# GpSimd's port work waits for planned VectorE work, LayerNorm statistics in larger groups, and a new order, in a spectral filter with a product-key expert layer

## The chip, the cores and the metric

One core of a Trainium2 chip runs the kernel. The metric is device microseconds of one execution, the median of several runs. A profiled execution gives the trace; its engines are PE (TensorE, with PEld for its weight loads), DVE (VectorE), ACT (ScalarE), POOL (GpSimd) and SP (SyncE, which issues the DMAs).

## The reference

```python
def _A_ref(x, w_r, w_i):
    X = rfft2(x, axes=(-2, -1))
    X = X * (w_r + 1j * w_i)
    return irfft2(X, s=(S, D), axes=(-2, -1))

def _B_ref(x, w_q, k1, k2, u, v):
    q = einsum("nd,dhc->nhc", x, w_q)
    s1 = einsum("nhd,ed->nhe", q[..., :dk], k1)
    s2 = einsum("nhd,ed->nhe", q[..., dk:], k2)
    # best key of each half for each head, K = 1
    i1, i2 = argmax(s1), argmax(s2)
    e = i1 * E + i2
    g = softmax over the one chosen score
    act = gelu(einsum("nd,nhkd->nhk", x, u[e]))
    return einsum("nhk,nhk,nhkd->nd", g, act, v[e])

xn = layernorm(x, axis=-1)
out = x + _A_ref(xn, w_r, w_i) + _B_ref(xn, w_q, k1, k2, u, v)
```

Here it is shortened. S = 2048 rows of D = 576; 32 heads, dk = 128, E = 8 keys in each half, 64 experts. All is float32.

## The kernel before

The 2048 rows lie in 16 tiles of 128. The kernel has these stages; the names are those that the trace shows, a tile name with several purposes is told.

*Statistics and forward DFT over rows, 16 tiles.* `ln(t, n)` makes the mean and variance of `n` tiles: BN_STATS on two halves of 288 columns (`st`) and an aggregate (`mv`) on VectorE, or, for the five tiles in `SA`, two passes over `XN` on ACT. Then ACT takes the square root for the whole group, VectorE its reciprocal, and one Newton step follows in three instructions, in `rr`: with a group of one or two tiles as three TENSOR_SCALAR for each tile, one column wide; with a group of more than two as three SCALAR_TENSOR_TENSOR for all its columns. Before the change the groups are of one, one and then seven times two tiles. `folds(t)` folds each row onto itself, two sums and differences of 289 columns (`t`) and then folds of 145 and 288 columns (`A`, whose tile is `A2`), on VectorE and GpSimd; ACT makes `Rs`, the row transform scaled by the tile's `rr`, and `yl`, a copy of some columns. `dft128(t)` multiplies `A` and `yl` by `Rs` on TensorE, and ACT copies the result to `AB` and `ABL`; a last difference for `ABL` is VectorE's.

*The folded keys.* `fold_part` reduces w_q with the keys, 32 tiles `w` of 576 KB that stream through five buffers; TensorE multiplies each by `KP`. These matmuls stand between those of the first stage and after them.

*The rest of the spectral branch.* `d_fwd` and `s_fwd` finish the forward transform (`c`, `s`), `s_mul(g)` multiplies by the weights: two products from PSUM on VectorE (`t<-banks,wx,Wt`), sums `y` on GpSimd, the high half `yh` on ACT, the low half `yh<-y,yh` on GpSimd, and `yl` on ACT. `s_inv(g)` is the inverse over rows, in 16 parts, and `d_inv(t)`, `fin(t)` the inverse over columns and the sum of both branches.

*The expert branch.* `x_t(r)` loads and scales `xT`, in two halves, the low one on VectorE or GpSimd; `scores(r)`, `route(r)` and `combine(r)` make the scores of two tiles, find the best key (`mx`, `w`, `MT` on VectorE) and the expert's weight (`MT`, `CZ` on GpSimd). `allmax` makes a scale from all partitions, through TensorE and an `mxr` on VectorE.

*What sets the order.* `body` doesn't issue instructions as it meets them. `_Engine` records each into a `_Plan`; `add` notes its planned cost, what it depends on, and in `op.port` whether it uses the port that VectorE and GpSimd are taken to share: every GpSimd instruction with an input, and a VectorE instruction with two inputs in SBUF or a copy or TENSOR_SCALAR from SBUF to SBUF. `forward` then plans: engine by engine it takes, of the instructions that are ready, the one with the highest priority, and lets only one user of the port run at a time. The priorities are a table, `RANK`, with one number for each recorded piece of work, 1319 before and 1284 after. `issue` calls the recorded functions in the planned order, so every instruction has the trace line of that call, L540 (L542 after). Each engine takes its own instructions in that order; between engines only data holds them. SyncE issues the DMAs, in that order too.

```python
    LOADS = ((0, 2), (2, 2), (4, 4), (8, 4), (12, 4))
```

These are the pieces in which `x` comes in, in tiles: first tile, count. They are the same before and after.

Of the kernel before, what the change touches and what calls it, by code (L numbers as in the profile page):

```python
# [32 lines left out]
def _consts():  # L33
# [102 lines left out]
    859, 1293, 1261, 1295, 1300, 1304, 1298, 1260, 593, 475, 479, 478, 895, 1174, 1177, 1005, 868, 805, 590,  # L136
    1187, 555, 893, 762, 927, 588, 543, 587, 892, 558, 410, 526, 537, 991, 728, 1049, 1022, 781, 857, 236,
    509, 1211, 758, 1168, 419, 658, 982, 981, 488, 1184, 957, 636, 1219, 985, 835, 218, 255, 943, 926, 986,
    679, 561, 722, 620, 611, 628, 862, 300, 709, 1026, 1079, 710, 517, 1042, 594, 1114, 1136, 1208, 856, 631,
    897, 319, 321, 880, 1266, 365, 1274, 723, 1169, 727, 888, 860, 915, 138, 145, 838, 858, 474, 606, 433,  # L140
    1011, 583, 626, 579, 815, 609, 373, 894, 342, 407, 343, 748, 445, 941, 1061, 1217, 655, 798, 973, 90, 189,
    741, 896, 415, 470, 1210, 1170, 356, 1220, 1037, 944, 178, 115, 913, 1013, 402, 673, 1244, 293, 751, 235,
    760, 922, 642, 601, 598, 354, 640, 610, 368, 299, 1178, 674, 1085, 416, 1267, 1252, 157, 314, 1202, 1110,
    1016, 731, 1151, 369, 1289, 494, 1086, 1032, 287, 317, 1138, 242, 198, 1082, 1108, 401, 666, 1247, 1130,
    1120, 816, 495, 597, 392, 1155, 530, 539, 965, 1097, 1087, 831, 869, 1175, 961, 186, 162, 219, 227, 199,
    1109, 1071, 1088, 570, 779, 1183, 1044, 306, 291, 1286, 847, 216, 372, 998, 371, 914, 1100, 1124, 1221,
    1056, 384, 763, 524, 566, 571, 387, 1212, 569, 318, 1215, 607, 480, 596, 463, 267, 483, 501, 667, 689,
    417, 1119, 1222, 386, 843, 575, 284, 175, 1111, 656, 533, 535, 577, 580, 261, 1066, 1053, 1281, 776, 546,
    338, 367, 333, 337, 545, 481, 1095, 1040, 366, 1272, 700, 531, 323, 266, 1041, 527, 891, 484, 840, 619,
    678, 615, 618, 536, 326, 269, 962, 1259, 390, 786, 828, 827, 1190, 809, 1065, 1265, 435, 425, 428, 599,  # L150
    540, 427, 426, 1080, 948, 1029, 547, 632, 1195, 845, 308, 116, 789, 792, 693, 1018, 1076, 604, 613, 396,
    884, 271, 32, 57, 311, 310, 329, 257, 156, 1189, 273, 500, 440, 1280, 756, 106, 1067, 97, 817, 270, 518,
    442, 456, 498, 1307, 1314, 952, 1309, 901, 1291, 1294, 1292, 1305, 767, 614, 247, 721, 379, 1299, 208,
    1303, 1205, 1301, 281, 1296, 521, 1297, 73, 1306, 394, 1229, 160, 1232, 355, 877, 1171, 459, 883, 890,
    1150, 210, 1310, 324, 1149, 209, 1283, 229, 1312, 105, 1248, 91, 1246, 165, 1250, 232, 904, 563, 882, 336,
    560, 265, 237, 1245, 1131, 989, 225, 681, 250, 950, 221, 1161, 58, 796, 233, 1179, 11, 1034, 919, 829,
    974, 477, 441, 214, 516, 204, 514, 278, 176, 378, 854, 173, 1023, 823, 234, 461, 790, 172, 783, 341, 476,
    1126, 289, 1139, 813, 253, 272, 254, 1268, 169, 898, 1256, 1092, 344, 1239, 429, 1009, 334, 292, 777, 161,
    268, 1165, 812, 550, 361, 1207, 1240, 395, 1050, 240, 376, 141, 765, 629, 328, 305, 617, 552, 670, 348,
    573, 239, 1159, 803, 900, 572, 899, 933, 578, 554, 553, 842, 397, 352, 231, 263, 163, 353, 262, 1253, 984,  # L160
    264, 109, 936, 290, 983, 1311, 312, 450, 801, 1308, 1209, 799, 761, 1313, 750, 680, 773, 1302, 844, 1039,
    720, 807, 657, 302, 804, 918, 430, 104, 103, 102, 100, 1288, 13, 154, 1132, 638, 639, 313, 1129, 616, 222,
    230, 970, 223, 806, 309, 205, 260, 1104, 1199, 246, 1135, 301, 244, 248, 834, 1060, 512, 602, 872, 1121,
    468, 431, 403, 486, 454, 833, 1101, 1064, 89, 93, 92, 1255, 203, 940, 277, 1007, 276, 586, 411, 1015, 771,
    811, 1198, 362, 249, 224, 695, 1063, 1269, 754, 283, 256, 393, 770, 715, 707, 641, 711, 1141, 1271, 1, 4,
    1069, 422, 1047, 385, 1096, 841, 1001, 1033, 1006, 1083, 787, 251, 228, 785, 932, 243, 325, 94, 1146, 968,
    226, 887, 213, 279, 280, 1287, 136, 132, 129, 127, 121, 126, 449, 1185, 755, 744, 574, 1193, 954, 589,
    1081, 1273, 643, 1200, 902, 96, 1181, 171, 177, 380, 282, 351, 295, 258, 259, 1073, 1036, 1249, 742, 824,
    5, 0, 938, 886, 1270, 1070, 955, 346, 917, 978, 556, 874, 423, 404, 1012, 977, 170, 168, 375, 340, 349,
    339, 595, 511, 976, 1162, 942, 793, 928, 3, 2, 906, 660, 207, 193, 206, 994, 374, 238, 327, 110, 303, 820,  # L170
    1290, 80, 88, 81, 79, 59, 153, 627, 1218, 649, 582, 653, 464, 544, 1062, 1000, 1238, 1194, 956, 1137, 152,
    775, 381, 167, 496, 331, 1106, 513, 399, 1014, 725, 1031, 1243, 724, 691, 133, 1197, 735, 1204, 1206, 621,
    697, 646, 335, 534, 360, 747, 759, 716, 714, 851, 992, 949, 1254, 245, 1052, 307, 830, 510, 489, 447, 708,
    706, 797, 538, 448, 1241, 174, 1123, 1214, 128, 87, 86, 1264, 1213, 275, 485, 166, 608, 668, 1318, 149,
    130, 124, 1231, 122, 123, 729, 907, 1167, 460, 444, 740, 418, 929, 947, 1285, 1234, 1004, 912, 52, 1057,
    414, 150, 591, 451, 873, 520, 482, 1230, 652, 732, 567, 622, 519, 101, 99, 951, 1019, 347, 939, 802, 692,
    971, 832, 1038, 794, 1107, 1164, 492, 462, 1075, 1228, 412, 83, 712, 452, 644, 696, 528, 525, 737, 694,
    931, 733, 1051, 191, 33, 1003, 357, 77, 82, 146, 1115, 769, 60, 499, 76, 562, 358, 1237, 117, 95, 190,
    202, 201, 197, 988, 1116, 1020, 1098, 585, 1224, 1196, 1142, 1024, 1276, 676, 808, 960, 113, 969, 75, 140,
    766, 389, 654, 388, 457, 434, 635, 634, 746, 1074, 1117, 84, 44, 630, 1226, 1172, 911, 1017, 1058, 662,  # L180
    605, 600, 1021, 1166, 453, 1284, 772, 664, 885, 144, 78, 505, 800, 1227, 879, 446, 432, 734, 1089, 909,
    1133, 503, 85, 413, 1182, 1192, 188, 114, 98, 1203, 866, 184, 532, 187, 1160, 1143, 108, 1242, 134, 151,
    288, 65, 135, 768, 810, 934, 975, 703, 1275, 1277, 865, 875, 1258, 1102, 853, 995, 37, 1030, 1046, 111,
    504, 472, 743, 881, 304, 274, 633, 739, 424, 749, 548, 1282, 139, 753, 1235, 1316, 1103, 1025, 469, 1257,
    522, 1145, 107, 112, 502, 864, 458, 690, 1093, 1223, 945, 684, 730, 719, 780, 69, 1233, 1068, 837, 192,
    147, 119, 814, 612, 64, 467, 120, 663, 542, 62, 55, 61, 54, 53, 143, 63, 867, 788, 958, 471, 846, 523,
    515, 1002, 819, 1154, 1027, 848, 964, 45, 778, 1090, 158, 757, 581, 736, 1216, 1262, 1263, 1043, 980,
    1077, 1099, 861, 1315, 764, 559, 466, 493, 871, 491, 159, 1173, 1191, 487, 1176, 437, 686, 541, 726, 738,
    1122, 717, 704, 155, 164, 74, 72, 46, 71, 70, 997, 1188, 1201, 465, 1225, 568, 473, 1140, 1112, 398, 497,
    1054, 923, 1078, 421, 196, 67, 1158, 252, 822, 391, 1317, 529, 551, 370, 320, 405, 345, 200, 142, 1186,  # L190
    508, 791, 420, 795, 889, 905, 996, 687, 406, 752, 294, 675, 443, 490, 1279, 1278, 35, 36, 818, 1045, 438,
    821, 924, 34, 56, 935, 377, 946, 1094, 937, 38, 15, 436, 1028, 718, 42, 47, 993, 439, 920, 1091, 921, 41,
    40, 637, 972, 1251, 39, 31, 903, 400, 603, 930, 659, 26, 27, 698, 1127, 1113, 43, 25, 1008, 702, 908, 870,
    705, 24, 23, 699, 990, 910, 211, 22, 825, 359, 576, 685, 623, 66, 68, 999, 1156, 1163, 30, 28, 826, 688,
    1153, 925, 564, 10, 148, 322, 1134, 1152, 17, 16, 713, 316, 315, 624, 1128, 7, 6, 1236, 1055, 1147, 8, 9,
    878, 651, 650, 683, 1059, 14, 12, 863, 1144, 1035, 20, 21, 1180, 855, 682, 661, 1118, 181, 179, 876, 1125,
    1148, 19, 180, 625, 565, 701, 1010, 849, 50, 49, 669, 979, 967, 51, 29, 836, 506, 507, 584, 784, 183, 131,
    549, 953, 959, 212, 48, 1157, 1048, 557, 1084, 774, 125, 182, 409, 966, 963, 18, 118, 648, 455, 852, 672,
    592, 1072, 220, 330, 987, 839, 137, 185, 408, 383, 382, 677, 671, 217, 215, 665, 1105, 916, 297, 296, 850,
# [1069 lines left out]
```

## Time and profile before

| | before |
|---|---|
| median of 3 runs | 222.05 us (221.85 to 222.1) |
| the profiled execution | 222.02 us |
| its span, first to last instruction | 220.1 us |
| granted TensorE clock | 0.992 |
| busy: PE, DVE, ACT, POOL | 194.9, 187.4, 130.5, 115.0 us |
| DMA: bytes | 48.12 MB |

A row of the trace names the line, the engine, the operation, what is written from what, and the shape; `x8` counts instructions. A timeline row has the start and the time from the first start to the last end, with the releaser of the idle time before it in brackets. Instructions overlap on an engine, so a group's time can be shorter than the sum of its instructions, and the distance between two starts tells what one more of them takes.

### The profile page before, as it was taken

How to read it: one execution, taken by the hardware profiler on the slowest of the kernel's cores; microseconds unless marked ns; L12 is line 12 of the kernel's file. 1: busy time of each engine (PE TensorE's matmuls, PEld its weight loads, DVE VectorE, ACT ScalarE, POOL GpSimd, SP SyncE). 2: the span in 40 equal slices, each digit the busy share in tenths (PEclk: the TensorE clock that was granted, in tenths of full speed). 3: DMA queues.
4: the chain of work that ended last, by engine and by line, in shares of the span. 5: the costliest groups of instructions: out<-in, count | busy, mean ns of one | idle time of the engine just before them, and what ended most of it. 6: DMA issues, size and time to landing. Idle time of an engine off the chain costs nothing.

```text
span 220.1 us, 6024 instructions
## 1 busy us (share of the span) xinstructions
PE 194.9 (89%) x2324; PEld 131.4 (60%) x2324; DVE 187.4 (85%) x457; ACT 130.5 (59%) x308; POOL 115.0 (52%) x153
## 2 busy tenths in 40 slices
PE   0179978989899999999999999969989999999990
PEld 0168557667656775657467465446555568877860
DVE  1999999971784967874899999999999999999980
ACT  2267989898857895849627934955635532213320
POOL 4644653602509840673416634867737239568760
PEclk9999999999999999999999999999999999999996
DMA  6999999999999999998224260201000000575466
GB/s 206 394 429 416 331 416 348 312 360 362 389 415 344 420 409 418 418 442 311 91 81 123 103 190 0 60 3 42 33 3 1 0 4 0 134 183 121 114 153 165
DMA packets 17020, 48.12 MB, mean 219 GB/s; under 512 B 2144, under 2 KB 8544, under 8 KB 16224
## 3 DMA queue, kind: packets, MB, share of 16 engines
q1 hardware_dynamic: 16992, 47.74, 61.1%
q8 instruction: 18, 0.29, 0.5%
q14 instruction: 10, 0.08, 0.1%
HBM read 43.01 MB, written 4.72 MB: 217 GB/s over the span
## 4 chain that ended last, share of the span: by engine, by line
PE 57%; DVE 29%; ACT 4%; issue 3%; DMA 3%; POOL 0%; ACTq 0%; DVEq 0%
PE banks L540 57%; DVE t L540 6%; DVE w L540 4%; DVE MT L540 4%; DVE A L540 3%; DVE st L540 2%; DVE rr L540 2%; DVE ABL L540 2%; DMA XN<-in_x_dram 2%; DVE AB L540 1%; ACT xT L540 1%; DMA w<-in_wq_dram 1%; DVE mx L540 1%; ACT xf L540 1%; DVE mm__96 L540 1%
## 5 line engine op out<-in xcount | busy, mean ns | idle before, releaser
L540 PE MATMUL banks<-MU,xT 128*128 128x512 f16 x192 | 45.7, 379 | 0.0
L540 PE MATMUL banks<-c,AB 128*128 128x145 f16 (+2 forms) x320 | 37.8, 252 | 0.0
L540 POOL TENSOR_TENSOR A<-t 128x287 f32<-128x287 f32 (+2 forms) x42 | 29.5, 722 | 15.6 <-DVE t L540 10.3
L540 POOL TENSOR_TENSOR y<-t,t 128x289 f32<-128x289 f32 x32 | 23.2, 748 | 22.7 <-DVE t L540 22.1
L540 PEld LDWEIGHTS <-xT 128*128 128x128 f16 x224 | 20.7, 98 | 23.2 <-issue 0.9
L540 DVE SCALAR_TENSOR_TENSOR t<-banks,wx,Wt 128x578 f32<-128x578 f32 x32 | 24.2, 810 | 3.9 <-PE banks L540 3.7
L540 POOL TENSOR_TENSOR yh<-y,yh 128x578 f16<-128x578 f32 x16 | 22.8, 1436 | 8.4 <-ACT yh L540 6.7
L540 PE MATMUL banks<-Rs,yl 128*99 128x128 f32 x64 | 12.0, 321 | 14.3 <-ACT Rs L540 11.8
L540 POOL TENSOR_TENSOR xT<-xf,xT 128x640 f16<-128x640 f32 x10 | 14.0, 1402 | 14.5 <-ACT xf L540 13.5
L540 ACT ACTIVATE AB<-banks 128x512 f32<-128x512 f32 (+1 forms) x32 | 18.8, 591 | 2.1 <-PE banks L540 1.8
L540 PEld LDWEIGHTS banks<-Rs,yl 128*99 128x99 f32 x64 | 8.6, 186 | 19.0 <-ACT Rs L540 14.2
L540 PE MATMUL banks<-w,KP 128*32 128x288 f32 x256 | 19.7, 414 | 0.1
L540 ACT ACTIVATE yh<-banks 128x290 f32<-128x290 f32 (+1 forms) x16 | 7.3, 458 | 20.8 <-PE banks L540 20.7
L540 PE MATMUL banks<-c,ABL 99*128 99x289 f16 (+1 forms) x64 | 18.8, 298 | 0.4 <-DVE ABL L540 0.4
L540 PEld LDWEIGHTS banks<-c,AB 128*128 128x128 f32 x128 | 17.9, 190 | 1.2 <-issue 0.5
L540 PE MATMUL banks<-Rs,A 128*128 128x128 f32 x128 | 18.5, 299 | 0.0
L540 DVE TENSOR_REDUCE MT<-w 128x128 bf16<-128x896 bf16 (+1 forms) x16 | 18.1, 1136 | 0.0
L540 PE MATMUL banks<-A,s 64*64 64x289 f32 x256 | 18.0, 411 | 0.0
L540 PEld LDWEIGHTS banks<-Rs,A 128*128 128x128 f32 x128 | 17.4, 214 | 0.9 <-issue 0.9
L540 PEld LDWEIGHTS <-AB 128*128 128x128 f16 x192 | 17.2, 147 | 0.1
L540 ACT ACTIVATE xT<-xf,bx 128x640 f16<-128x640 f32 x16 | 13.0, 821 | 5.6 <-PE banks L540 5.5
L540 POOL TENSOR_TENSOR t<-XN 128x289 f32<-128x289 f32 x14 | 11.9, 864 | 8.4 <-DVE A L540 4.2
(127 smaller groups left out, 417.8 us busy)
## 6 DMA issues: line engine op xcount, KB each, us to landing
w<-in_wq_dram SPq DMA_DIRECT2D x32, 576.0 KB, 6.8
xf<-in_xT_dram SPq DMA_DIRECT2D x16, 320.0 KB, 5.6
Wt<-in_W_dram SPq DMA_DIRECT2D x8, 578.0 KB, 6.7
out_dram<-XN SPq DMA_DIRECT2D x32, 144.0 KB, 2.5
XN<-in_x_dram SPq DMA_DIRECT2D x3, 1154.0 KB, 10.7
s<-in_s_dram SPq DMA_DIRECT2D x16, 192.0 KB, 5.1
XN<-in_xd_dram SPq DMA_DIRECT2D x2, 1152.0 KB, 9.7
XN<-in_xd_dram SPq DMA_DIRECT2D x1, 2304.0 KB, 12.3
```

The costliest lines, as they stand in the source:

```text
L540: fn(*[x.place() if isinstance(x, _Ps) else x for x in args], **{k: x.place() if isinstance(x, _Ps) else x for k, x in kw.items()})
```

## The change

Three things change.

The groups of `ln` become those of `LOADS`. With them go the instructions that work on a group: the square root, the reciprocal, and, where a group has four tiles, the Newton step.

`issue` keeps, for each VectorE instruction that it has issued, the planned end with some time added. For each GpSimd instruction that uses the port it looks for the last VectorE instruction with such an end no later than its own planned start, and adds a dependency on it. It adds no second dependency on the same instruction.

`RANK` is replaced as a whole, so that the order on each engine is another.

```diff
 RANK = (
-    859, 1293, 1261, 1295, 1300, 1304, 1298, 1260, 593, 475, 479, 478, 895, 1174, 1177, 1005, 868, 805, 590,
...
+    464, 1220, 901, 1223, 1261, 1268, 1219, 1221, 391, 444, 431, 691, 894, 879, 874, 922, 835, 890, 883, 839,
...
 )
-    def issue(self):
+    def issue(self, tc):
...
+        sync = mybir.DependencyInfo(mybir.DependencyClass.Sync, mybir.DependencyReason.DATA)
+        queue, held = [], None
         for i in order:
-            for fn, args, kw in ops[i].calls:
-                fn(*[x.place() if isinstance(x, _Ps) else x for x in args],
-                   **{k: x.place() if isinstance(x, _Ps) else x for k, x in kw.items()})
+            o = ops[i]
+            for fn, args, kw in o.calls:
+                ins = fn(*[x.place() if isinstance(x, _Ps) else x for x in args],
+                         **{k: x.place() if isinstance(x, _Ps) else x for k, x in kw.items()}).ins
+            if o.eng == "vector":
+                queue.append((start[i] + o.cost + 225, ins))
+            elif o.eng == "gpsimd" and o.port:
+                first = [v for t, v in queue if t <= start[i] + 30]
+                if first and first[-1] is not held:
+                    held = first[-1]
+                    tc.add_manual_dep(ins, held.name, sync, reason="port")
...
-        plan.issue()
+        plan.issue(tc)
...
-    for t, n in ((0, 1), (1, 1), (2, 2), (4, 2), (6, 2), (8, 2), (10, 2), (12, 2), (14, 2)):
+    for t, n in ((0, 2), (2, 2), (4, 4), (8, 4), (12, 4)):
         ln(t, n)
         for i in range(t, t + n):
             folds(i)
```

Counted over the program, VectorE has 382 rows of such an order instead of 412, ACT 266 instead of 275, and TensorE and GpSimd the same work.

The first instructions on VectorE, from the first that waits for `x`. The numbers in the names are buffers: `A2_0` and `A2_1` are here tiles 0 and 1.

Before:

```order
L540 TENSOR_TENSOR t1_1_99<-XN_67 128x289
L540 BN_STATS st_0_97<-XN_67 128x6 x2
L540 BN_AGGR mv_87<-st_0_97 128x2
L540 BN_STATS st_0_97<-XN_67 128x6
L540 RECIPROCAL rr_86<-rr_86 128x1
L540 TENSOR_TENSOR A2_1_101<-t1_1_99 128x145
L540 TENSOR_SCALAR rr_86<-rr_86 128x1
L540 TENSOR_TENSOR A2_1_101<-t1_1_99 128x145
L540 TENSOR_SCALAR rr_86<-mv_87,rr_86 128x1
L540 TENSOR_TENSOR t1_0_98<-XN_67 128x289
L540 TENSOR_SCALAR rr_86<-rr_86 128x1
```

After the change, from the same place up to the first pair's `rr`:

```order
L542 TENSOR_TENSOR t_0_98<-XN 128x289
L542 BN_STATS st_97<-XN 128x6 x2
L542 BN_AGGR mv<-st_97 128x2
L542 TENSOR_TENSOR A_1_101<-t_1_99 128x145
L542 BN_AGGR mv<-st_97 128x2
L542 BN_STATS st_97<-XN 128x6
L542 RECIPROCAL rr<-rr 128x2
L542 BN_STATS st_97<-XN 128x6
L542 TENSOR_SCALAR rr<-rr 128x1 x2
L542 TENSOR_TENSOR t_1_99<-XN 128x289
L542 BN_AGGR mv<-st_97 128x2
L542 TENSOR_SCALAR rr<-mv,rr 128x1 x2
```

Ahead of the rows shown stand four BN_STATS, a fold of 145 columns and an aggregate, and after them two more TENSOR_SCALAR on `rr`. The Newton step of the first tile stood after two BN_STATS; it now stands after eight, for two tiles together. The first such step over four tiles, that of tiles 4 to 7, comes some 35 rows later.

The first matmuls on TensorE, from the first on. `Rs_0` and `Rs_1` are two buffers that even and odd tiles take in turn, `A2_0` to `A2_3` four that go round the tiles, and `w_0` is the first tile of the folded keys.

Before:

```order
L540 MATMUL banks_66<-Rs_0_104,yl_0_106 99x2x8x8 x2
L540 MATMUL banks_66<-Rs_0_104,A2_0_100 128x128 x4
L540 MATMUL banks_66<-Rs_1_105,yl_1_107 99x2x8x8 x2
L540 MATMUL banks_66<-Rs_0_104,yl_0_106 99x2x8x8 x2
L540 MATMUL banks_66<-Rs_0_104,A2_2_102 128x128 x4
L540 MATMUL banks_66<-Rs_1_105,A2_1_101 128x128 x4
L540 MATMUL banks_66<-w_0_119,KP_73 32x288 x4
L540 MATMUL banks_66<-Rs_1_105,yl_1_107 99x2x8x8 x2
L540 MATMUL banks_66<-Rs_1_105,A2_3_103 128x128 x4
```

After:

```order
L542 MATMUL banks_66<-Rs_1_105,yl_1_107 99x2x8x8 x2
L542 MATMUL banks_66<-Rs_0_104,yl_0_106 99x2x8x8 x2
L542 MATMUL banks_66<-Rs_1_105,A2_1_101 128x128 x4
L542 MATMUL banks_66<-Rs_0_104,A2_0_100 128x128 x4
L542 MATMUL banks_66<-Rs_1_105,yl_1_107 99x2x8x8 x2
L542 MATMUL banks_66<-w_0_119,KP_73 32x288 x4
L542 MATMUL banks_66<-Rs_1_105,A2_3_103 128x128 x4
L542 MATMUL banks_66<-Rs_0_104,yl_0_106 99x2x8x8 x2
L542 MATMUL banks_66<-Rs_1_105,yl_1_107 99x2x8x8 x2
L542 MATMUL banks_66<-Rs_0_104,A2_2_102 128x128 x4
L542 MATMUL banks_66<-Rs_1_105,A2_1_101 128x128 x4
```

Tiles 0, 1 and 3 come first; the ninth row is the `yl` of tile 5, and stands ahead of the tenth, the four matmuls of tile 2. Before, all of tile 2 stood ahead of tiles 3, 4 and 5.

GpSimd in the middle of the inverse over rows, with the engines whose semaphores each instruction waits for.

Before:

```order
L540 TENSOR_TENSOR y_0_131<-t1_0_98,t2_0_108 128x289 [waits DVE_49,Pool_49]
L540 TENSOR_TENSOR y_0_131<-t2_0_108,t1_0_98 128x289
L540 TENSOR_TENSOR CZ_80<-MT_79,CZ_80 128x2x64 [waits Activation_49]
L540 TENSOR_TENSOR MT_79<-MT_79,mk_70 128x128
L540 TENSOR_TENSOR yh_0_133<-y_0_131,yh_0_133 128x578 [waits PE_49,Activation_49]
L540 TENSOR_TENSOR y_1_132<-t2_1_109,t1_1_99 128x289 [waits DVE_49]
L540 TENSOR_TENSOR y_1_132<-t1_1_99,t2_1_109 128x289
L540 TENSOR_TENSOR yh_1_134<-y_1_132,yh_1_134 128x578 [waits Activation_49]
```

After:

```order
L542 TENSOR_TENSOR y_0_131<-t2_0_108,t1_0_98 128x289 [waits DVE_49,Pool_49]
L542 TENSOR_TENSOR y_0_131<-t1_0_98,t2_0_108 128x289 [waits DVE_49]
L542 TENSOR_TENSOR CZ_80<-MT_79,CZ_80 128x2x64 [waits DVE_49]
L542 TENSOR_TENSOR MT_79<-MT_79,mk_70 128x128 [waits DVE_49]
L542 TENSOR_TENSOR yh_0_133<-y_0_131,yh_0_133 128x578 [waits DVE_49,Activation_49]
L542 TENSOR_TENSOR y_1_132<-t1_1_99,t2_1_109 128x289 [waits DVE_49]
L542 TENSOR_TENSOR y_1_132<-t2_1_109,t1_1_99 128x289 [waits DVE_49]
L542 TENSOR_TENSOR yh_1_134<-y_1_132,yh_1_134 128x578 [waits DVE_49,PE_49,Activation_49]
```

The order here is nearly the same. Each row now names VectorE: of GpSimd's 143 computing instructions 52 waited for VectorE before, and 128 do after.

127 rows, old and new, of the table RANK are left out of this document.

## The prediction

> **What bounds the kernel now.** The sums of the page and its chain of waits come first.
>
> ```profile
> PE 194.9 (89%) x2324; PEld 131.4 (60%) x2324; DVE 187.4 (85%) x457; ACT 130.5 (59%) x308; POOL 115.0 (52%) x153
> PE 57%; DVE 29%; ACT 4%; issue 3%; DMA 3%; POOL 0%; ACTq 0%; DVEq 0%
> ```
>
> TensorE is busy for 194.9 of 220.1 us and VectorE for 187.4; the chain runs over both and never over GpSimd. An average hides the stages, so the busy time by windows is next (columns after the window: its length, then PE, PEld, DVE, ACT, POOL, clock, DMA share, GB/s).
>
> ```profile
> 10.00:22.90 12.90, 11.57 (x67) 10.16 (x68) 12.86 (x56) 8.40 (x26) 6.69 (x14) 1.00 1.02 422
> 22.90:52.30 29.40, 25.89 (x257) 18.54 (x256) 25.40 (x101) 26.32 (x74) 10.92 (x17) 1.00 0.95 351
> 50.00:110.00 60.00, 58.93 (x722) 37.91 (x721) 41.07 (x93) 44.87 (x88) 28.59 (x29) 1.00 0.94 367
> 110.00:205.00 95.00, 91.69 (x1149) 59.08 (x1147) 94.28 (x173) 47.16 (x113) 56.99 (x70) 1.00 0.25 66
> ```
>
> Four stages: some 10 us without a matmul (the first row of the next fence); the statistics, folds and the DFT of 16 tiles up to 52.3, where VectorE is full until 22.9 and ACT (26.32 of 29.40) is the tightest engine behind it; 50 to 110, TensorE full; 110 to 205, VectorE full (94.28 of 95) with TensorE idle 3.3. The waits of TensorE by what it waits for:
>
> ```profile
> PE banks L540 <- ACT Rs L540: 11.8, 3, 10.1
> PE banks L540 <- DVE mxr L540: 2.9, 4, 1.9
> ```
>
> The 10.1 is the start, the 1.9 a wait for an `mxr` late in the kernel. Both parts of the change aim at places on the path: the statistics at the first 52 us, the waits at 110 to 205. From 50 to 110 TensorE has 1.07 us of idle, so what the first stage loses is hardly won back there.
>
> **The change, part by part.** *Instructions saved.* The old groups of one and two tiles issue 48 small TENSOR_SCALAR and 9 reciprocals; the new ones issue 12 and 5, and 9 SCALAR_TENSOR_TENSOR over four columns.
>
> ```profile
> L540 DVE TENSOR_SCALAR rr<-rr 128x1 f32<-128x1 f32 x32 | 5.3, 201 | 0.1
> 39.76 0.32 DVE L540 TENSOR_SCALAR rr<-mv,rr 128x1 f32<-128x1 f32 x2
> 40.00 0.32 DVE L540 TENSOR_SCALAR rr<-rr 128x1 f32<-128x1 f32 x2
> ```
>
> The mean of 201 ns overlaps with its neighbour: two take 0.24 us from start to start, 0.12 each. So 36 x 0.12 = 4.3 us go, and four reciprocals at some 0.07. The added nine have no row of their shape; they lie between that reciprocal and one and a third TENSOR_SCALAR, 0.07 to 0.16, and I take 0.1: 0.9 back. VectorE is lighter by about 3.7 us in a stage where it is busy for 12.86 + 25.40 of 42.3 us, and ACT by four square roots.
>
> *The first matmul.* It needs the scale `rr` of tile 0 or 1, then ACT's `Rs` and `yl`. The rows that price the instructions on the way, each by the distance to the next start:
>
> ```profile
> 4.65 0.46 DVE L540 TENSOR_TENSOR t<-XN 128x289 f32<-128x289 f32 x1 [3.68 <-DMA XN<-in_x_dram]
> 8.31 0.46 DVE L540 BATCH_NORM_STATS2 st<-XN 128x6 f32<-128x288 f32 x1
> 8.68 0.45 DVE L540 TENSOR_TENSOR A<-t 128x288 f32<-128x288 f32 x1
> 9.04 0.20 DVE L540 BATCH_NORM_AGGREGATE mv<-st 128x2 f32<-128x12 f32 x1
> 9.16 0.94 DVE L540 TENSOR_TENSOR t<-XN 128x289 f32<-128x289 f32 x1
> 38.32 0.30 DVE L540 TENSOR_TENSOR A<-t 128x145 f32<-128x145 f32 x1
> 38.53 0.41 DVE L540 TENSOR_TENSOR ABL<-banks,ABL 33x256 f16<-33x256 f32 x1
> 38.87 0.14 DVE L540 RECIPROCAL rr<-rr 128x2 f32<-128x2 f32 x1
> 10.06 1.18 PE L540 MATMUL banks<-Rs,yl 128*99 128x128 f32 x4 [10.06 <-ACT Rs L540]
> ```
>
> BN_STATS 0.37, AGGREGATE 0.12, a fold of 288 columns 0.36, of 289 some 0.38, of 145 0.21, `ABL` 0.34, reciprocal 0.07. In the new order eight BN_STATS (3.0), four AGGREGATE (0.5), two folds of 289 (0.8), two of 145 (0.4), a reciprocal and six TENSOR_SCALAR (0.8) stand from 4.65 up to the last `rr` of the first pair: 10.1. ACT then makes two `Rs` and a `yl`, about 0.35 each: first matmul at 11.2 instead of 10.06.
>
> *The group of four.* In TensorE's new order the matmuls of tile 5 stand ahead of the last of tile 2, and TensorE takes its queue in order. Tile 5's `rr` comes out of the group of tiles 4 to 7, behind 18 BN_STATS (6.7), 9 AGGREGATE (1.1), eight folds of 289 (3.0), five of 288 (1.8), seven of 145 (1.5), two `ABL` (0.7), 12 TENSOR_SCALAR (1.4), three reciprocals and three of the new ones (0.5): 16.7 us after 4.65, so 21.4 without a single wait, and with `Rs` and signals about 22.2. What TensorE has to do before it is priced by these rows:
>
> ```profile
> 11.03 1.92 PE L540 MATMUL banks<-Rs,A 128*128 128x128 f32 x8
> 16.29 3.17 PE L540 MATMUL banks<-Rs,A 128*128 128x128 f32 x16
> 20.01 0.68 PE L540 MATMUL banks<-Rs,yl 128*99 128x128 f32 x4
> 20.52 1.06 PE L540 MATMUL banks<-Rs,A 128*128 128x128 f32 x8
> 21.65 0.68 PE L540 MATMUL banks<-Rs,yl 128*99 128x128 f32 x4
> 23.84 1.18 PE L540 MATMUL banks<-w,KP 128*32 128x288 f32 x16
> 24.95 1.16 PE L540 MATMUL banks<-Rs,A 128*128 128x128 f32 x8
> 29.07 1.23 PE L540 MATMUL banks<-Rs,yl 128*99 128x128 f32 x8 [1.85 <-ACT yl L540]
> 30.14 1.95 PE L540 MATMUL banks<-Rs,A 128*128 128x128 f32 x16
> 52.49 0.30 PE L540 MATMUL banks<-c,ABL 99*128 99x289 f16 x1
> ```
>
> A tile takes 1.64 (20.01 to 21.65), of it 0.5 for `yl`; one `w` takes 0.56 (23.84 to 24.95 is two). Up to tile 5 there are tiles 0, 1 and 3, the `yl` of tile 2 and one `w`, ending at about 17. So TensorE idles some 5 us there, where today it idles 1.33 in the whole of 10 to 22.9. The stage holds 16 x 1.64 + 16 x 0.56 = 35.2 us of such work; 6.0 are done by 22.2, the other 29.2 end at 51.4 if not one gap is left; today the next stage's first matmul starts at 52.49. Two things add to that. The matmuls after the first long idle are slow: eight of `A` take 1.92 and sixteen 3.17, later 1.06 and 1.95, though the granted clock reads 1.00 in all of these windows; after the gap of 1.85 at 29.07 nothing is slow. A gap of 5 lies between: 0 to 2.1 us (0.9 + 1.2), and I take 1.0. The Trainium skill, "TensorE: Matmul & The Clock Gate", in its part on the HAM clock gate, has the array at half clock until some 3.4 us of sustained work, and one run there fell back 5.2 us after the last matmul; the doubled rows agree, the column of the clock doesn't show it, and by that page a gap of 5 is on the edge: if it counts it costs about 1.7, an estimate from 3.4 us at half speed, and the sum below would be 223.8. And today's gaps from 22.9 to 52.3 are 29.40 - 25.89 = 3.5; VectorE's 3.7 us fill part of them, ACT's 90% doesn't change, and I take half, 1.7. Its end, 51.4 + 1.0 + 1.7 = 54.1, is later by **+1.6 us**, with the ends -1.1 (no gap, no slow matmul) and +4.5.
>
> *The waits.* GpSimd's work on SBUF stretches VectorE's and the other way. These rows show it (the last is of the chain, the two before it of GpSimd):
>
> ```profile
> 117.04 0.41 DVE L540 TENSOR_TENSOR w<-w,MT 128x512 bf16<-128x512 bf16 x1
> 130.25 0.60 DVE L540 TENSOR_TENSOR w<-w,wt 128x896 bf16<-128x896 bf16 x1
> 139.53 1.82 DVE L540 TENSOR_TENSOR w<-w,wt 128x896 bf16<-128x896 bf16 x1
> 141.28 1.50 DVE L540 TENSOR_TENSOR w<-w,MT 128x512 bf16<-128x512 bf16 x1
> 139.46 1.41 POOL L540 TENSOR_TENSOR xT<-xf,xT 128x640 f16<-128x640 f32 x1
> 140.82 1.68 POOL L540 TENSOR_TENSOR yh<-y,yh 128x578 f16<-128x578 f32 x1
> 145.15 4.33 PE banks L540 x44
> ```
>
> The same two instructions take 0.60 and 0.41 alone, 1.82 and 1.50 while `xT` and `yh` run: 2.3 us, in the chain just ahead of the `mxr` for which TensorE waits 1.9. The new wait makes GpSimd start such work only when the VectorE instructions planned before it are done. It changes nothing for a VectorE instruction that arrives while GpSimd is already at work: that one is still stretched. Bounds: nothing, if all collisions are of the second kind, and 3.3 us, all of TensorE's idle in 110 to 205. I take half of the one wait that the rows tie to a collision: **-1.0 us**. What waits behind a held GpSimd instruction is GpSimd's whole queue, `y`, `yh`, `CZ`, `xT`, and behind these ACT's `yl` and the inverse matmuls. GpSimd is busy for 57 of 95 us, so most of it is covered; I put **+0.5** on it, between 0 and the 4.9 of the first rival. The matmuls and transfers of the later stages are the same in number, but for one W tile that now goes after the last `w`.
>
> Sum: 222.02 (profiled run, 220.1 of it span) + 1.6 - 1.0 + 0.5 = **223.1**; the median shown is 222.05, so the base is the same.
>
> **The rivals.** (1) *GpSimd held behind VectorE's backlog*, 110 to 205: VectorE is full there, so it can be late against the plan by its commonest long instruction.
>
> ```profile
> L540 DVE SCALAR_TENSOR_TENSOR t<-banks,wx,Wt 128x578 f32<-128x578 f32 x32 | 24.2, 810 | 3.9 <-PE banks L540 3.7
> POOL y L540 <- DVE t L540: 22.1, 8, 8.2
> POOL yh L540 <- ACT yh L540: 6.7, 5, 3.6
> ```
>
> Six pairs of inverse matmuls wait for a `yh` each, 0.81 later: 4.9 in place of 0.5, so 227.5. For it: VectorE has no slack. Against: today `yh` waits for ACT at five of 16 places only, and `y` is made well ahead. It decides once `yh` ends after TensorE's previous work. (2) *The first stage gains*, which ends on the other side: the lighter VectorE lets everything behind 22.2 run without gaps and without slow matmuls, -1.1 for +1.6: 220.4, or less if tile 5's scale comes before 21.4. For it: VectorE is full to 22.9 and loses 3.7. Against: ACT's 90%. (3) *The collisions go altogether*: -3.3 and no hold, 222.02 + 1.6 - 3.3 = 220.3. For it: 1.9 us stand at one such place. Against: only one side waits. (4) *The waits change nothing*, since the instructions named are long done: 223.6. Here the Trainium skill, "SBUF — State Buffer", section "Who interferes with whom", says that whoever issues first has the shared ports for the whole instruction and the other blocks; the stretched rows agree, and by it only half of the collisions can be ordered from GpSimd's side.
>
> **How the numbers follow.** Forecast 0.40, rival (1) 0.18, (2) 0.22, (3) 0.13, (4) 0.07. About 0.2%, 0.44 us, can be told from no change here. The forecast's own range, 221.4 to 225, is cut as 0.31 slower, 0.06 same, 0.03 faster; (1) and 0.06 of (4) are slower, (2) and (3) faster but for 0.01 that falls to same, as does 0.01 of (4). Slower 0.55, same 0.08, faster 0.37. The range leaves out half of (1) and the case in which (2) and (3) come together (217.6): 218.8 to 226.8.
>
> **What would show it.** The first matmul near 11.2. A gap of 4 to 6 us on TensorE between 16 and 23, named by `Rs` or `yl`, with slow `A` matmuls behind it. TENSOR_SCALAR on `rr` down to 12, and VectorE's busy time in 10 to 52 down by 3 to 4. The first matmul of the next stage after 53. From 110 to 205: no 1.82 and 1.50 under an `xT` and a `yh`, the wait for `mxr` near 1, and GpSimd's waits for VectorE longer than the 22.1 that it has for `y`. The prediction is wrong if TensorE has no such gap before 23, if the next stage starts before 52, or if `yh` is waited for by VectorE and TensorE's idle in 110 to 205 grows.

## The result, and the profile after

| | before | changed |
|---|---|---|
| median | 222.07 us (221.85 to 222.6, 4 runs) | 216.33 us (215.94 to 216.88, 4 runs) |
| ratio | | 0.974, interval 0.9713 to 0.9767 |
| span of the profiled execution | 220.1 us | 214.2 us |
| granted TensorE clock | 0.992 | 0.987 |

The change makes the kernel faster by 2.6%, about 5.7 us. The forecast was 223.1 us, slower, with a range from 218.8: the time lies below it, and on the other side.

The sums of the changed kernel and its busy time by windows (length, PE, PEld, DVE, ACT, POOL, clock, DMA share, GB/s); the last window ends at 199 and not 205, since the changed kernel is six microseconds ahead there:

```profile
PE 191.7 (89%) x2324; PEld 131.4 (61%) x2324; DVE 178.3 (83%) x426; ACT 129.8 (61%) x304; POOL 112.9 (53%) x153
```

```profile
10.00:22.90 12.90, 8.62 (x52) 7.60 (x53) 12.21 (x50) 10.71 (x31) 7.20 (x12) 0.92 1.01 421
22.90:52.30 29.40, 28.51 (x275) 21.06 (x274) 21.58 (x71) 25.57 (x68) 11.75 (x16) 0.98 0.98 372
50.00:110.00 60.00, 59.10 (x716) 38.38 (x715) 42.77 (x94) 43.65 (x88) 28.98 (x29) 1.00 0.93 358
110.00:199.00 89.00, 88.61 (x1141) 58.99 (x1141) 87.82 (x170) 47.61 (x113) 54.42 (x70) 1.00 0.25 67
```

VectorE is busy for 9.1 us less in all. TensorE's idle (length less PE) is 4.3 us in the first of these windows, where it was 1.3, and 0.9 in the second, where it was 3.5. In the last window it is 0.39 in 89 us, where it was 3.31 in 95. The waits of TensorE:

```profile
PE banks L542 <- ACT yl L542: 14.7, 3, 10.9
PE banks L542 <- DVE t L542: 0.9, 2, 0.5
PE banks L542 <- DVE AB L542: 0.4, 1, 0.4
```

The wait of 1.9 us for an `mxr` is gone. TensorE's timeline (start, duration, instruction, idle before and its releaser) shows the first stage:

```profile
10.92 2.03 PE L542 MATMUL banks<-Rs,yl 128*99 128x128 f32 x8 [10.92 <-ACT yl L542]
...
16.90 1.16 PE L542 MATMUL banks<-Rs,A 128*128 128x128 f32 x8
21.16 2.03 PE L542 MATMUL banks<-Rs,yl 128*99 128x128 f32 x8 [3.10 <-ACT yl L542]
22.98 2.60 PE L542 MATMUL banks<-Rs,A 128*128 128x128 f32 x16
...
51.96 0.30 PE L542 MATMUL banks<-c,ABL 99*128 99x289 f16 x1
```

The first matmul is later, at 10.92, and there is a gap of 3.1 us with slow matmuls behind it; yet the next stage starts at 51.96 instead of 52.49. From there to the end it took 220.1 - 52.5 = 167.6 us before and takes 214.2 - 52.0 = 162.2 now. So 0.5 of the 5.9 us was won by 52 us, and 5.4 behind it. Where VectorE's time went, by groups from 105 to 205 us: before the change

```profile
L540 DVE TENSOR_TENSOR w<-w,MT 128x512 bf16<-128x512 bf16 x16 | 9.7, 618 | 0.0
L540 DVE TENSOR_TENSOR w<-w,wt 128x896 bf16<-128x896 bf16 x8 | 6.1, 762 | 0.1
L540 DVE TENSOR_TENSOR MT<-MT 128x128 f32<-128x128 int32 x7 | 3.0, 425 | 0.1
L540 DVE TENSOR_TENSOR al<-wx,mk 128x16 f32<-128x16 f32 x1 | 1.3, 1272 | 0.0
```

and after it

```profile
L542 DVE TENSOR_TENSOR w<-w,MT 128x512 bf16<-128x512 bf16 x16 | 6.4, 412 | 0.0
L542 DVE TENSOR_TENSOR w<-w,wt 128x896 bf16<-128x896 bf16 x8 | 5.6, 699 | 0.0
L542 DVE TENSOR_TENSOR MT<-MT 128x128 f32<-128x128 int32 x8 | 2.2, 279 | 0.0
L542 DVE TENSOR_TENSOR al<-wx,mk 128x16 f32<-128x16 f32 x1 | 0.2, 171 | 0.0
```

All four are TENSOR_TENSOR with both inputs in SBUF. Sixteen `w<-w,MT` now have a mean of 412 ns, which is the time of one alone; the `al`, sixteen columns wide, took 1.27 us and takes 0.17. The four groups together lose 20.1 - 14.4 = 5.7 us. They are those that lose most; others with two inputs in SBUF got longer, `MT<-MT,fm` from a mean of 283 to 339 ns for one. To count all of them, take the stretch of an instruction as its time less the shortest one of its form in any run's trace. Over all two-input instructions of VectorE that start after 105 us the stretch sums to 7.8 us before the change and to 2.8 after it: 5.0 us went, and some is left, as in two of the eight `w<-w,wt`, which take 0.81 and 1.11 us.

### The profile page after: what moved, and what is told of

Read it like the earlier page. It is cut to its first block, busy times and chain, and to the rows that moved or that the text cites. A ratio compares the mean times of both kernels' runs of the same rounds, so it can differ in the third digit from the quotient of the medians.

```text
span 214.2 us, 6027 instructions
## 1 busy us (share of the span) xinstructions
PE 191.7 (89%) x2324; PEld 131.4 (61%) x2324; DVE 178.3 (83%) x426; ACT 129.8 (61%) x304; POOL 112.9 (53%) x153
## 4 chain that ended last, share of the span: by engine, by line
PE 54%; DVE 32%; issue 5%; ACT 2%; POOL 2%; DMA 2%; DVEq 0%; POOLq 0%
PE banks L542 54%; DVE t L542 8%; DVE MT L542 5%; DVE A L542 4%; DVE st L542 3%; DVE w L542 2%; DVE AB L542 2%; DMA XN<-in_x_dram 2%; DVE ABL L542 2%; POOL t L542 2%; DVE mx L542 1%; DVE mm__96 L542 1%; DVE rr L542 1%; ACT yl L542 1%; POOL y L542 1%
## 5 line engine op out<-in xcount | busy, mean ns | idle before, releaser
L542 PE MATMUL banks<-MU,xT 128*128 128x512 f16 x192 | 45.2, 379 | 0.0
L542 POOL TENSOR_TENSOR A<-t 128x289 f32<-128x289 f32 (+2 forms) x42 | 26.5, 649 | 14.7 <-PE banks L542 5.6
L542 POOL TENSOR_TENSOR yh<-y,yh 128x578 f16<-128x578 f32 x16 | 20.8, 1309 | 10.2 <-ACT yh L542 6.8
L542 PE MATMUL banks<-Rs,yl 128*99 128x128 f32 x64 | 11.2, 319 | 15.0 <-ACT yl L542 14.7
L542 PE MATMUL banks<-w,KP 128*32 128x288 f32 x256 | 20.3, 415 | 0.2 <-DMA w<-in_wq_dram 0.2
L542 POOL TENSOR_TENSOR t<-XN 128x289 f32<-128x289 f32 x14 | 13.1, 942 | 10.9 <-DVE A L542 5.3
L542 PEld LDWEIGHTS banks<-Rs,A 128*128 128x128 f32 x128 | 16.7, 207 | 3.3 <-issue 2.3
L542 PE MATMUL banks<-A,s 64*64 64x289 f32 x256 | 17.5, 410 | 0.0
L542 DVE TENSOR_TENSOR ABL<-banks,ABL 33x256 f16<-33x256 f32 x32 | 13.0, 410 | 5.0 <-ACT ABL L542 4.7
```

What stands on the lines that cost most here:

```text
L542: ins = fn(*[x.place() if isinstance(x, _Ps) else x for x in args], **{k: x.place() if isinstance(x, _Ps) else x for k, x in kw.items()}).ins
```

## The experiments

All ratios stand against the kernel before, run on the same chip each time (medians of 222.06 to 222.28). "The waits" are GpSimd's new dependencies.

**Waits out, and waits alone.** The changed kernel without its waits, then the kernel before with nothing but the waits.

```diff
-            elif o.eng == "gpsimd" and o.port:
+            elif o.eng == "gpsimd" and o.port and False:
```

> The changed kernel with the new waits of GpSimd left out; its groups and its order stay. Theory W (the waits take the collisions of GpSimd with VectorE out of 110 to 180 us, worth 4 to 5 us; groups and order give the other 1 to 2): 220.3 to 221.3 us, and the VectorE instructions w<-w,MT and w<-w,wt stretched again as before the change (means near 0.6 and 0.78 us). Theory O (the new order alone keeps the two apart, the waits are met anyway): 216.3 within 0.6.

The second kernel is the one before, with its own `RANK` and groups and the new `issue`.

> The kernel before with the waits alone: old groups, old order. Theory W: the collisions go here too, so 3 to 4 us faster than before, 218 to 219.2 us, with TensorE's idle of 3.3 us in 110 to 205 down to about 1. Theory O: 222 within 0.6, or slower, since the old order has GpSimd's work wait where it did not before.

Without the waits: 221.3 us, ratio 0.9967 (0.9935 to 0.9999), so groups and order by themselves give 0.3%, just clear of none. Its ten runs spread from 220.19 to 222.71, more than those of the kernel before; the last section says what goes with it. The waits alone: 216.28 us, 0.9743 (0.9726 to 0.9761), the whole gain of the change. Theory O, by which the new order keeps the engines apart, is out. Theory W holds, and for the second kernel its size was too small by 1.7 us or more. VectorE and then GpSimd in the kernel with the waits alone, at the place of the collision that the prediction quoted:

```profile
137.36 0.63 DVE L543 TENSOR_TENSOR w<-w,wt 128x896 bf16<-128x896 bf16 x1
137.90 0.42 DVE L543 TENSOR_TENSOR w<-w,MT 128x512 bf16<-128x512 bf16 x1
```

```profile
138.16 1.43 POOL L543 TENSOR_TENSOR xT<-xf,xT 128x640 f16<-128x640 f32 x1 [0.82 <-DVE w L543]
139.55 1.28 POOL L543 TENSOR_TENSOR yh<-y,yh 128x578 f16<-128x578 f32 x1
```

GpSimd now stands idle for 0.82 us until the first `w` is done, and starts the `xT` 0.17 us after the end of that `w`; then the two `w` take 0.63 and 0.42 where they took 1.82 and 1.50, and `yh` takes 1.28 where it took 1.68. Both engines gain. In this trace the stretch after 105 us is 3.2 us, and without the waits in the changed kernel it is 9.1.

**Which waits.** The changed kernel with only the waits of GpSimd's work planned after 100 us, then with only those planned before it; and the kernel before with the late ones.

```diff
-            elif o.eng == "gpsimd" and o.port:
+            elif o.eng == "gpsimd" and o.port and start[i] >= 100e3:
```

> The changed kernel with only those waits whose GpSimd instruction is planned to start after 100 us. Theory W, as it was worked out for 110 to 180 us: 216.3 within 0.6. If the waits matter in the first 100 us as well: 217 to 219. Theory O: 216.3.

> The changed kernel with only those waits whose GpSimd instruction is planned to start before 100 us. Theory W: 220.3 to 221.3, as without any waits. Theory O: 216.3 within 0.6.

> The kernel before with only those new waits whose GpSimd instruction is planned after 100 us. If the 1.6 to 1.9 us that all waits gained up to the first s_fwd in the kernel before come from the early waits and stay to the end: 218.0 within 0.5. If the late part makes up for it: 216.3. If the late waits work only together with the early ones: above 219.

In the changed kernel the late waits give everything: 216.21 us, 0.9728 (0.9704 to 0.9752). The early ones give nothing: 221.51, 0.9973 (0.9949 to 0.9997). In the kernel before, the late ones give 218.17, 0.9829 (0.9813 to 0.9845), and by the difference from all waits (216.28) the remaining 1.9 us come from the early ones, which were not run alone there. So the early collisions cost time with the old groups and order alone, and the late ones with both. The changed kernel has early collisions too: with all waits the stretch up to 55 us is 4.5 us, with the late ones alone 6.1, and the time is the same. In the changed kernel VectorE is busy for 21.58 of 29.40 us from 22.9 on, and for 87.82 of 89 in the late stage.

**One collision.** The kernel before with two waits, those of the `xT` and the `yh` of the prediction's fence.

```diff
-            elif o.eng == "gpsimd" and o.port:
+            elif o.eng == "gpsimd" and o.port and 136.5e3 <= start[i] < 139e3:
```

> The kernel before with two waits alone, those of the xT and the yh that collide with two w instructions at 139 to 143 us. Theory S (each collision costs what it stretches VectorE by, and the total gain is their sum): 220.0 to 220.6, which is the 1.9 us that TensorE waited for this mxr. Theory K (this wait is the knot, all that follows falls into place): 216.5 to 217.5. Theory R (the time comes back as another wait): 222.2 within 0.4.

220.66 us, 0.9939 (0.9923 to 0.9956): 1.5 us, at the edge of theory S. In the trace the `mxr` behind it comes at 142.87 instead of 144.82, 2.0 us earlier; then a part is lost again, because the next collision is a new one. VectorE, then GpSimd:

```profile
145.61 1.34 DVE L543 TENSOR_TENSOR w<-w,MT 128x512 bf16<-128x512 bf16 x1
```

```profile
145.38 1.29 POOL L543 TENSOR_TENSOR yh<-y,yh 128x578 f16<-128x578 f32 x1
```

The same pair of instructions did not meet before (that `w` took 0.42 at 147.32). Who meets whom is a matter of tenths of a microsecond, and moving one place shifts all behind it. A wait at each place mends that.

**How exact the wait must be.** In the changed kernel the wait is put on VectorE instructions planned to end later, or earlier, than those of the change.

```diff
-                first = [v for t, v in queue if t <= start[i] + 30]
+                first = [v for t, v in queue if t <= start[i] + 830]
```

> The changed kernel, but each port instruction of GpSimd waits for VectorE instructions planned to end up to 0.8 us later than those it waits for now. It prices the term of a held GpSimd. If GpSimd's slack covers it: 216.3 within 0.6. By the prediction's first rival (yh late by some 0.8 at six pairs of inverse matmuls): 219 to 221.

> As the run with the longer hold of 0.8 us, but only for GpSimd's instructions planned after 100 us. It prices the prediction's first rival by itself. If the hold cost there came from the first stage and from 50 to 110 (where the trace has some 2.3 us of it): 218.5 to 219.7. If it is all in the late stage: 221 to 222. If the late stage has slack: 216.3 within 0.5.

> The changed kernel with each wait moved to a VectorE instruction planned to end 0.3 us later than now. If GpSimd's slack covers a small hold: 216.3 within 0.6. If every such delay is paid, in proportion to the 5.6 us for 0.8: 218 to 218.8.

> The changed kernel with each wait moved to a VectorE instruction planned to end 0.5 us earlier than now, so that GpSimd may start that much sooner. If the exact instruction matters, since the VectorE instruction just ahead is the one that GpSimd's work collides with: 218.5 to 221. If a rough order is enough: 216.3 within 0.6.

| wait put | median, us | ratio, interval |
|---|---|---|
| 0.8 us later | 221.97 | 0.9993 (0.998 to 1.0007) |
| 0.8 us later, after 100 us alone | 219.95 | 0.9886 (0.9862 to 0.991) |
| 0.3 us later | 216.67 | 0.9756 (0.9734 to 0.9777) |
| as in the change | 216.33 | 0.974 (0.9713 to 0.9767) |
| 0.5 us earlier | 218.38 | 0.982 (0.9798 to 0.9843) |
| none | 221.3 | 0.9967 (0.9935 to 0.9999) |

A hold that is 0.8 us too long costs as much as the waits bring. The run with the late hold shows two things: TensorE waits for GpSimd, 1.2 us at three places of the late stage, and collisions come back (means of 477 for 412 and 746 for 699; the stretch after 105 us is 5.4 us for 2.8). That GpSimd's held work now runs into the next VectorE instruction is the likely reason.

```profile
PE banks L542 <- POOL yh L542: 0.5, 1, 0.5
PE banks L542 <- POOL A L542: 0.4, 1, 0.4
...
PE banks L542 <- POOL CZ L542: 0.3, 1, 0.3
```

```profile
L542 DVE TENSOR_TENSOR w<-w,MT 128x512 bf16<-128x512 bf16 x16 | 7.4, 477 | 0.0
L542 DVE TENSOR_TENSOR w<-w,wt 128x896 bf16<-128x896 bf16 x8 | 6.0, 746 | 0.0
```

A wait that lets GpSimd go 0.5 us earlier loses 2 us of the 5, and the stretch after 105 us is 6.7 us. With 0.3 us later the interval overlaps with that of the change: that much hold costs nothing that can be told.

**The saved instructions.** The changed kernel with the Newton step of its groups of four made tile by tile, in the same places.

```diff
             V.scalar_tensor_tensor(r, q, 96.0, r, op0=OP.add, op1=OP.mult)
+            for op, f in zip(plan.ops[-3:], (lambda r, q, v: (q, r, r, -32.0), lambda r, q, v: (q, v, 1e-5, q),
+                                             lambda r, q, v: (r, q, 96.0, r))):
...
+                op.calls = [(V.obj.tensor_scalar, f(rr[:, 0, i:i + 1], rr[:, 3, i:i + 1], mv[:, i, 1:2]),
+                             dict(op0=ops[0], op1=ops[1])) for i in range(t, t + n)]
             return
```

The three recorded operations keep their places in the plan, and each then issues one TENSOR_SCALAR for each of its four tiles.

> The changed kernel with the Newton step of the groups of four made tile by tile again, as 36 TENSOR_SCALAR in the places of 9 SCALAR_TENSOR_TENSOR; nothing else moves. It puts 27 x 0.12 = 3.2 us back on VectorE in the first stage. If VectorE sets the end of that stage: 218.5 to 219.5. If only tile 5's scale counts (nine more instructions ahead of it, 1.0 us): 217.3. If ACT sets it and VectorE's saving was worth nothing: 216.3 within 0.4.

218.19 us, 0.9829 (0.9807 to 0.9852): 27 instructions cost 1.9 us, between the expectations that VectorE sets the whole stage and that only tile 5's scale counts. TensorE's idle from 22.9 to 52.3 is 2.1 us again, where the change has 0.9:

```profile
22.90:52.30 29.40, 27.26 (x253) 19.69 (x254) 24.14 (x91) 23.66 (x66) 12.08 (x16) 1.00 0.95 341
```

**Tile 2 ahead of tile 5.** The changed kernel with tile 5's `yl` matmuls moved behind those of tile 2 on TensorE.

```diff
+        late = [i for i in ten(5) if order.index(i) < last]
+        order = [i for i in order[:last + 1] if i not in late] + late + order[last + 1:]
```

Here `ten(t)` are the tensor operations of `dft128(t)` in the planned order, and `last` is the place of the last of tile 2.

> The changed kernel with the matmuls of tile 2 put ahead of those of tile 5 on TensorE; nothing else moves. If TensorE's gap of 3.1 us before tile 5 sets the end of the first stage: 1.0 to 1.3 us of work go into the gap, 215.0 to 215.4, and the first matmul of the next stage starts near 50.9. If ACT or VectorE sets that end: 216.3 within 0.4, with the gap of 3.1 cut but others later.

216.2 us, 0.973 (0.9709 to 0.9751): no difference. The gap is as long, and its releaser the same:

```profile
21.10 0.68 PE L548 MATMUL banks<-Rs,yl 128*99 128x128 f32 x4 [3.05 <-ACT yl L548]
```

It is tile 2's own `yl` that TensorE waits for. The changed kernel's trace shows why. VectorE, then ACT:

```profile
16.05 0.43 DVE L542 TENSOR_TENSOR A<-t 128x288 f32<-128x288 f32 x1
...
20.08 0.10 DVE L542 SCALAR_TENSOR_TENSOR rr<-rr 128x4 f32<-128x4 f32 x1
...
20.40 0.30 DVE L542 TENSOR_TENSOR A<-t 128x145 f32<-128x145 f32 x1
```

```profile
20.73 0.37 ACT L542 ACTIVATE yl<-A 128x198 f32<-128x198 f32 x1 [0.23 <-DVE A L542]
```

In VectorE's new order tile 2's fold of 288 columns stands at 16.05, and its last fold of 145 only at 20.40, behind the statistics of tiles 4 to 7 and amid their Newton step; its `yl` follows at 20.73. The same queue that makes the group's statistics makes this fold late.

**Small groups and fewer instructions.** The kernel before with the waits, and in its groups of two the Newton step for both columns at once, in the place of the first of the two; and the same with GpSimd's smallest instructions left without a wait.

```diff
+        if n == 2:
+            r, q, v = rr[:, 0, t:t + 2], rr[:, 3, t:t + 2], mv[:, t:t + 2, 1]
+            both = ((q, r, -32.0, r, OP.mult), (q, v, 1e-5, q, OP.add), (r, q, 96.0, r, OP.add))
...
+        for i, j, call in self.pairs:
+            if where[j] < where[i]:
+                i, j = j, i
+            ops[i].calls, ops[j].calls = [call], []
...
-            elif o.eng == "gpsimd" and o.port:
+            elif o.eng == "gpsimd" and o.port and o.cost > 200:
```

The last line belongs to the second of the two kernels alone.

> The kernel before with the waits, its small groups and its order, but in each group of two tiles the Newton step is made for both columns at once: 3 SCALAR_TENSOR_TENSOR in the places of the first of each 6 TENSOR_SCALAR, so 21 instructions fewer on VectorE in the first stage. Theory C (what the larger groups of the change win is the count of instructions on VectorE, 1.9 us for 27; what they lose is the later start of tile 0 and tile 2's late fold): 21/27 of 1.9 = 1.5 us faster than the waits alone, 214.4 to 215.2, and the first matmul stays near 10. Theory D (with small groups the first stage is set by ACT or the loads and not by VectorE's count): 216.3 within 0.4.

> The same, but GpSimd's small instructions (KP, mv and the cast of the identity, each planned below 0.2 us) get no new wait. In the kernel before with the waits, TensorE waited 1.1 us for a KP that was held by VectorE. If that wait is on the path: another 0.5 to 1.1 us faster than the run with the pairs. If it was covered: the same within 0.3.

215.8 us, 0.9709 (0.9693 to 0.9725), and 215.38 us, 0.9699 (0.968 to 0.9717). The pairs give 0.5 us on top of the waits alone instead of the 1.5 of theory C, and their intervals touch. Two things may stand against more; no run parts them. ACT is busy for 27.62 of 29.40 us, as the row shows; and the new instruction has two inputs in SBUF and collides itself. Its groups on VectorE, and one collision on VectorE and GpSimd:

```profile
22.90:52.30 29.40, 27.08 (x269) 19.91 (x268) 22.97 (x81) 27.62 (x75) 10.73 (x18) 1.00 0.99 372
```

```profile
L549 DVE SCALAR_TENSOR_TENSOR rr<-mv,rr 128x2 f32<-128x2 f32 x7 | 2.5, 362 | 0.1
```

```profile
27.37 0.72 DVE L549 SCALAR_TENSOR_TENSOR rr<-mv,rr 128x2 f32<-128x2 f32 x1
```

```profile
27.28 0.80 POOL L549 TENSOR_TENSOR t<-XN 128x289 f32<-128x289 f32 x1
```

Two columns take 0.72 us and end at 28.09, as GpSimd's `t` ends at 28.08; the shortest of the seven takes 0.14, so the seven lose 7 x (0.36 - 0.14) = 1.5 us. The TENSOR_SCALAR in its place had a mean of 0.20. Leaving the small GpSimd instructions free can't be told from no gain by the intervals; TensorE's wait for `KP`, 1.1 us in the kernel with the waits alone, is no longer in the trace of the kernel with the pairs either. The last of these kernels is the fastest of the study, 0.9 us below the changed one by the medians; its interval and that of the change overlap at 0.9713 to 0.9717.

## Why the prediction was wrong

*What bounds the kernel* was read rightly: TensorE and VectorE, VectorE full from 110 to 205. What follows from that was not carried through in the step on the waits.

*The waits, -1.0 us.* The step "I take half of the one wait that the rows tie to a collision" failed. The mechanism was right, and the size was off by five times: the waits are worth 221.3 - 216.33 = 5.0 us in the changed kernel and 222.25 - 216.28 = 6.0 in the one before. Of the 6.8 us between forecast and result some 4.5 lie here, the hold counted in. The one collision is worth 1.5, near its 1.9; the error was to stop at it. VectorE was busy for 94.28 of 95 us, so a stretch of it is hardly covered by anything, and it was the stretch of all two-input instructions that had to be summed: 7.8 us after 105 us, of which 5.0 went. The reason given for taking half, that a VectorE instruction which comes while GpSimd works is still stretched, may account for the 2.8 us that are left; but `w<-w,MT`, 5 of 16 of which were stretched, is back at 406 to 420 ns in all sixteen. The Trainium skill, "SBUF — State Buffer", section "Who interferes with whom", calls the ports that VectorE shares with GpSimd an exclusive lock and lets issue order decide who blocks; the trace agrees in the collision that ends 0.01 us after GpSimd's instruction. From it rival (4) drew that only half of the collisions can be ordered from GpSimd's side. The page doesn't speak of a half, and 5.0 of 7.8 us went: with the waits fewer of the two engines' instructions meet.

*The upper bound of 3.3 us* for the late stage, all of TensorE's idle there, was too low. From the first `c,ABL` matmul of `d_fwd` to the first of `d_inv` it took 175.56 - 52.49 = 123.1 us before and takes 169.92 - 50.88 = 119.0 with the waits alone, 4.0 less. TensorE's idle in that stretch went from 4.3 to 1.3 us, 3.0 less; the other 1.0 lies in time that the profile counts as busy. The ends of matmuls are modelled in it; what this part is, no run shows.

*The hold, +0.5 us*, was not measured by itself; it is in the 5.0, and 0.3 us more of it doesn't show. Rival (1) was no outcome. Its mechanism shows in part with 0.8 us more in the late stage: that costs 3.6 us, but TensorE waits for a `yh` only once, for 0.5, and not at six pairs.

*The first stage, +1.6 us.* It came out at -0.5 (51.96 for 52.49) in this execution, at -0.3 with the late hold (52.21), at +0.2 without the waits (52.71) and at +0.6 with the late waits alone (53.08): about nothing. With the Newton step by tile it was +1.6 (54.07). Its parts:

- First matmul 11.2: it was 10.92.
- A gap of 5 us up to 22.2, because tile 5 stands ahead of tile 2: the gap is 3.1 us, from 18.06 to 21.16, and the reason was wrong. Tile 2's own folds are late; the order of the two tiles on TensorE changes nothing, as the run with them exchanged shows.
- Slow matmuls after it, 1.0: they are there, 2.03 for 1.12 on eight `yl` and 2.60 for 1.95 on sixteen `A`, 1.6 us in the profiled execution. In the run with the Newton step by tile the same gap of 3.07 is followed by 1.46 and 1.95. The price varies.
- "I take half" of today's gaps of 3.5 from 22.9 on, 1.7: 0.9 were left. VectorE's saving was undervalued here; the run with the Newton step by tile puts 1.9 us on 27 of the instructions.
- The restart and the work behind it, 22.2 + 29.2: TensorE restarts at 21.16, and what it does until 51.96, less gaps and slowness, is 30.8 - 0.9 - 1.6 = 28.3 us.

Together: 1.0 for the restart, 0.9 for the work and 0.8 for the gaps, less 0.6 for the slow matmuls, is the 2.1 us from 54.1 to 51.96. No one of them turns the sign alone.

Groups and order together are worth 0.3% without the waits, with an interval from 0 to 0.65%, and nothing on top of them (216.28 and 216.33). The saved instructions are worth 1.9 us, so something loses as much: the later start, the gap and the slow matmuls are there to see, but no run takes them out one by one, and whether the groups or the new order bring the loss was not tried.

*The rivals.* (3), that the collisions go, is nearest to what happened, though 2.8 us of stretch are left. It was priced at 220.3, with 3.3 us of gain and the first stage at +1.6; the gain was 5.0, and the first stage came out about even. That puts the result near the case that the prediction left out of its range, (2) and (3) together at 217.6.

## What to carry to other kernels

Where an engine is full, sum the stretch of its instructions over all groups, mean less the time of one alone, and take that sum as the most that can be won; the place where another engine visibly waits is only one of the payments. A semaphore wait that holds GpSimd until the VectorE instruction just ahead is done won back most of it here, 5.0 of 7.8 us, but it has to name the right instruction: 0.5 us too early or 0.8 too late lost 2 us or more. Where VectorE isn't full, as from 22.9 to 52.3 us in the changed kernel, the early waits won nothing. Before a gap is explained by the order on the waiting engine, follow the operand of its first instruction back to where it is made.

## What the hardware showed that was not expected

In the collisions shown, a two-input VectorE instruction that meets a GpSimd instruction is not slowed in proportion: it ends with it, or less than its own short time later. Two columns took 0.72 us for 0.14 and ended 0.01 behind GpSimd's `t`; the sixteen of `al` took 1.27 for 0.17 and ended at 159.32, 0.03 behind a `yh`. So the price was the rest of GpSimd's instruction, and small instructions were no safer than large ones; two TENSOR_SCALAR, 0.24 us from start to start, can be cheaper than one SCALAR_TENSOR_TENSOR.

A gap on TensorE can be followed by slow matmuls and half the clock. The rows are of a window each (length, PE, PEld, DVE, ACT, POOL, clock, DMA share, GB/s), in this order: the changed kernel behind its gap of 3.1 us; the kernel before with the late waits, behind a gap of 1.86; the kernel before, behind its gap of 1.85 at the same place; the changed kernel with the early waits alone, behind the 2.04 us that it waits for an `mxr`; and the one without waits, behind 2.02 at the same place.

```profile
22.00:24.00 2.00, 2.00 (x11) 2.00 (x10) 1.72 (x8) 1.09 (x4) 0.83 (x2) 0.50 1.04 429
30.00:32.00 2.00, 2.00 (x11) 2.00 (x11) 1.97 (x9) 1.62 (x6) 0.86 (x3) 0.50 1.04 426
30.00:32.00 2.00, 2.00 (x19) 1.89 (x17) 1.97 (x9) 2.00 (x8) 0.93 (x3) 1.00 1.02 414
145.00:148.00 3.00, 3.00 (x17) 2.54 (x15) 3.00 (x8) 2.10 (x5) 1.75 (x2) 0.50 0.02 5
145.00:148.00 3.00, 3.00 (x32) 2.74 (x34) 3.00 (x7) 3.00 (x8) 2.40 (x2) 1.00 0.02 5
```

In the fourth row's stretch four `c,AB` matmuls take 1.17 us, in the fifth's 0.66. Gaps of the same length were followed by it in one execution and not in another. The Trainium skill, "TensorE: Matmul & The Clock Gate", in its part on the HAM clock gate, tells of a run that fell back 5.2 us after its last matmul; here it came after shorter gaps. The spread of the kernel without waits goes with the granted clock of its runs: 220.19 to 221.32 us at 0.984 to 0.992, and 222.43 to 222.71 at 0.976 or 0.977. So a collision that makes TensorE wait can cost a second time, in some executions. The gain of the waits isn't this alone: at 0.996 or more the kernel before took 221.75 to 221.97 us on that chip, and with nothing but the waits 216.28 to 216.72.
